# The head of an attention and gated feed-forward kernel, issued in one listed order on all engines

## The chip, the cores and the metric

The kernel runs on one core of one Trainium2 chip. The metric is the device time of the whole launch in microseconds, from the start of the program to its end, as the median of several executions. The core has five engines with a queue of instructions each: TensorE (PE in the profile, with its weight loads as PEld), VectorE (DVE), ScalarE (ACT), GpSimd (POOL) and SyncE (SP), which here issues DMAs. Each engine takes its own instructions in the order in which they stand in its queue, and semaphores hold an instruction until what it reads is there and what it overwrites is no longer needed. The order inside each queue is therefore part of the kernel.

## The reference

Attention with a causal window of 64 over 8 batches, 8 heads, 576 tokens and 64 channels, then a root-mean-square norm and a gated feed-forward layer on the 4608 tokens of 512 channels:

```python
scores = scale * np.matmul(q, k.transpose(0, 1, 3, 2))
rel = pos[:, None] - pos[None, :]
mask = (rel >= 0) & (rel < window)
scores = np.where(mask, scores, -1000000000.0)
...
attn = attn / (np.sum(attn, axis=-1, keepdims=True) + 1e-09)
return np.matmul(attn, v).astype(np.float32)
...
x = np.ascontiguousarray(attn_out.transpose(0, 2, 1, 3)).reshape(B * S, H * D)
rms = np.sqrt(np.mean(x * x, axis=-1, keepdims=True) + 1e-06)
xn = x / rms * rms_g
g = xn @ w_gate
silu = g * (1.0 / (1.0 + np.exp(-g)))
val = xn @ w_val
return (silu * val @ w_out).astype(np.float32)
```

w_gate and w_val have 512 x 1536 elements, w_out 1536 x 512, all f32.

## The kernel before

**Attention.** Two heads make a pair, so that there are 32 pairs, 4 in each batch. Pair n has the tiles q_n and kv_n (keys and values), which SP loads: kv_n by one DMA for the bulk (L348) and two for the last values (L361, L362). A pair's scores come in two parts g = 0 and 1 and two halves, one for each head: sc_n_g_0 and sc_n_g_1 (L397 to L401). Each half uses 64 rows of the PE array. DVE masks the scores and takes their maxima (L414, written to p and st), ACT takes the exponentials (L417), PE turns the weights (tr, L518), ACT or DVE copies them from PSUM (pt, L521 to L523), and PE multiplies them with the values (xp, L536). The result goes to xb. PSUM has one bank for scores, one for tr, two for xp and the widening products, and three (mo) for the feed-forward sums.

**Norm.** After batch 0's four pairs, the sums of squares (ssq) are added up on PE (tot, L773), ten short steps on DVE make inverse roots of them (rm, L791 and L828), and PE spreads these over partitions (rb, L852). DVE scales xb by them and by the weights gsb (L882), and writes xn (L886, L888).

**Feed-forward.** The 4608 tokens are 9 tiles of 512. A product of f32 accuracy is three f16 products of high and low parts (`three`, L976 to L979). Tile 0 runs expert_in(0, c) for the six chunks c of 256 columns: gate sums pg_0_j and value sums pv_0_j for j = 0 to 11, then th and h on ACT, DVE and POOL. expert_out(0) makes the output sums po_0 from h and w_out. Tiles 3 to 8 use a scheme of seven products (L1153).

**Weights.** They arrive as f32 (1 MB a chunk) in staging tiles st_0_c (gate), st_1_c (value) and st_o_c (w_out), issued on SP (L204) into three buffers. ACT makes two exponentials of the top byte (mp, mn, L217 and L218), PE adds them (pw, L226 and L227, with the constant `unit`), DVE puts the other bits in (wt, L229), so that the f32 value is rebuilt. Then come the maxima (top), a scale (n2, z, ws), and the split into high and low f16 parts (L238 to L248) on ACT, DVE and POOL. A staging buffer comes free when DVE's second wt step has read it.

**What sets the order.** SEQ (L1296) is "00 01 02 03 04 05 o0": the six chunks of tile 0, then its output stage o0. Attention of batch 0 (`first_batch`, L727) is written first; attention of batch 1, the widening and the first products of pair 8 are written as a plan of events that `advance` (L1355) calls as tile 0's steps go by. Up to o0 the compiler's own scheduler puts the instructions of each engine in order, by its model of durations. `behind` (L1276) adds edges to that: the parts in it may not be issued ahead of what was last written on the named engines. From o0 on (ORDERED, L46) `in_written_order` (L90) fixes the order on all five engines as it was written.

Of the kernel before, what the change touches and what calls it, by code (L numbers as in the profile page):

```python
# [62 lines left out]

@with_exitstack
def tile_window_attention_moe(
# [205 lines left out]
    def in_scale(c):  # L271
# [7 lines left out]
        nc.vector.tensor_scalar(r.bitcast(I32), n2.bitcast(I32), -0.5, RSQRT_SEED + 12.9 * 2.0**23, ALU.mult, ALU.add)
# [973 lines left out]
    def expert_out(t):  # L1253
        if t == 0:
            pos = [(ps_mo if k < 3 else ps_mi).tile([P, DM], F32, tag="mo" if k < 3 else "mi", name=f"po_0_{k}") for k in range(TT // P)]
            for c in range(NC):
                for k, po in enumerate(pos):
                    tick(Fraction(2, NC))
                    chunk_out(po, t, c, k, c == 0, c == NC - 1)
                    if c == NC - 1:  # L1260
                        store(po, t, k)
            return
        for k in range(TT // P):
            halves = 2 if t == NT - 1 and k == TT // P - 1 else 1
            for e in range(halves):
                es = slice(e * DM // halves, (e + 1) * DM // halves)
                po = (ps_mo.tile([P, DM], F32, tag="mo", name=f"po_{t}_{k}_{e}") if t < FIRST7 else banks[(0, 2, 5, 1)[(k + e) % 4]])[:, es]
                for c in range(NC):
# [4 lines left out]
                    chunk_out(po, t, c, k, c == 0, c == NC - 1, es)
                store(po, t, k, es)

    def behind(parts, engines):  # L1276

        last = {}
        for ins in nc.cur_bb.bb.instructions:
            last[ins.engine] = ins  # L1280
        with ExitStack() as order:
            for e in engines:
                order.enter_context(tc.issue_after(last[e.engine]))
            for part in parts:
                part()
# [145 lines left out]
```

## Time and profile before

| | us |
|---|---|
| median of 3 runs | 988.48 |
| lowest, highest run | 984.96, 990.56 |
| the profiled execution, whole time | 989.32 |
| the profiled execution, span of the profile | 987.2 |
| first output matmul of tile 0 (po_0_0) | 173.4 |

The page divides the span into 40 slices of 24.7 us. Each digit is the share of a slice in tenths; the first seven slices are what comes before o0:

```profile
PE   7778999999999999999999999999999999999998
PEld 5544445444445444588758875886588658847875
DVE  6676966877787775647674766576757645512540
ACT  5566877555544454356635663566366334413440
POOL 3333645487847675557665756675667222200210
PEclk9987999999999999999999999999999999999999
```

A timeline row reads: start, duration, engine, line, operation, output<-inputs with the tile's number left out, size, count, and in brackets the idle time of the engine ahead of it with what ended that time. A product of two f32 tiles is recorded as two matmuls. A windows row reads: start and end, length, busy time and count of each engine, the granted clock of PE as a share of full speed, the busy share of the DMA engines, and GB/s. A group's row ends with busy time, mean ns of one, and idle time ahead of the group with its causes. A row of waits reads: engine and waiting line, what it waited for, us in total, times, the longest. A row of the DMA part ends with the median us from issue to landing.

### The profile page before, as it was taken

The page shows a single profiled execution, that of the slowest core. Times are in us where ns is not written, and L with a number is a line of the kernel's source. Part 1 is how long each engine was busy: PE and PEld are TensorE (multiplying, and loading weights), DVE is VectorE, ACT ScalarE, POOL GpSimd, SP SyncE. Part 2 cuts the span into 40 slices and gives each one's busy share as a digit, 9 for nine tenths or more (in the row PEclk, how much of TensorE's full clock was granted, in tenths as well). Part 3 has the DMA queues.
Part 4 walks back from the last instruction along what each step waited for, and adds up shares of the span by engine and source line. Part 5 has one row for each costly group of instructions (what it writes and reads, how often), then busy time and mean ns, then how long its engine had stood idle before and what let it go on. Part 6 is the DMA issues. An engine that isn't in the chain of part 4 may idle for free.

```text
span 987.2 us, 20767 instructions
## 1 busy us (share of the span) xinstructions
PE 957.8 (97%) x7820; PEld 626.7 (63%) x7831; DVE 631.3 (64%) x1721; ACT 512.3 (52%) x1303; POOL 499.1 (51%) x634
## 2 busy tenths in 40 slices
PE   7778999999999999999999999999999999999998
PEld 5544445444445444588758875886588658847875
DVE  6676966877787775647674766576757645512540
ACT  5566877555544454356635663566366334413440
POOL 3333645487847675557665756675667222200210
PEclk9987999999999999999999999999999999999999
...
GB/s 289 179 95 219 115 255 84 59 160 36 153 124 105 164 213 155 33 147 207 298 35 146 212 294 34 146 219 290 31 197 186 137 33 193 202 76 107 140 8 35
DMA packets 81315, 143.42 MB, mean 145 GB/s; under 512 B 25792, under 2 KB 38336, under 8 KB 81216
## 3 DMA queue, kind: packets, MB, share of 16 engines
...
q8 instruction: 61, 1.00, 0.4%
q10 hardware_dynamic: 576, 1.18, 0.3%
...
HBM read 121.64 MB, written 20.45 MB: 144 GB/s over the span
## 4 chain that ended last, share of the span: by engine, by line
PE 88%; DVE 4%; ACT 2%; POOL 2%; DMA 2%; issue 1%; SPq 0%; POOLq 0%; ACTq 0%; DVEq 0%
PE bk L1153 29%; PE bk L977 6%; PE bk L978 6%; PE bk L979 6%; PE xp L536 5%; PE sc L401 4%; PE po L977 3%; PE po L978 3%; PE po L979 3%; PE pg L979 3%; PE pv L977 3%; PE pg L977 3%; PE pg L978 3%; PE pv L979 3%; PE pv L978 3%
## 5 line engine op out<-in xcount | busy, mean ns | idle before, releaser
L1153 PEld LDWEIGHTS <-wt 128*128 128x128 f16 x3024 | 295.2, 98 | 39.2 <-issue 2.8
L383 POOL TENSOR_TENSOR pm<-pm,st 32x288 f32<-32x288 f32 (+1 forms) x384 | 265.0, 690 | 71.4 <-DVE st L451 26.1
L1153 PE MATMUL bk<-xn,wt 128*128 128x256 f16 x1728 | 207.3, 273 | 0.5 <-DVE u L1223 0.5
L998 POOL TENSOR_TENSOR h<-th,h 128x512 f16<-128x512 f32 x78 | 93.8, 1203 | 170.0 <-ACT h L998 156.5
L1153 PE MATMUL bk<-wt,wt 128*128 128x256 f16 x1224 | 150.3, 273 | 0.3 <-ACT u L1173 0.3
L977 PE MATMUL bk<-wt,h 128*128 128x512 f16 (+1 forms) x300 | 111.3, 371 | 0.0
L978 PE MATMUL bk<-wt,h 128*128 128x512 f16 (+1 forms) x300 | 111.1, 370 | 0.0
L979 PE MATMUL bk<-wt,h 128*128 128x512 f16 (+1 forms) x300 | 111.1, 370 | 0.0
L417 ACT ACTIVATE pm<-pm,st 128x128 f32<-128x128 f32 (+1 forms) x216 | 83.9, 389 | 36.6 <-DVE st L414 35.7
L998 ACT CAST h<-th 128x512 f16<-128x512 f32 x94 | 57.9, 616 | 52.0 <-DVE th L1043 34.7
L1195 DVE SCALAR_TENSOR_TENSOR th<-th,bk 128x256 f32<-128x256 f32 x108 | 44.8, 415 | 50.8 <-ACT th L1185 50.3
L979 PEld LDWEIGHTS <-h 128*128 128x128 f16 x436 | 42.7, 98 | 49.6 <-issue 0.8
L977 PEld LDWEIGHTS <-h 128*128 128x128 f16 x436 | 43.0, 99 | 47.8 <-issue 3.1
L1185 ACT ACTIVATE th<-bk,hsc 128x256 f32<-128x256 f32 x108 | 47.9, 471 | 47.8 <-DVE bk L1219 28.4
L978 PEld LDWEIGHTS <-h 128*128 128x128 f16 x436 | 42.7, 98 | 44.7
L1216 DVE TENSOR_TENSOR bk<-bk,s 128x512 f32<-128x512 f32 x36 | 25.1, 696 | 69.0 <-PE bk L1153 48.4
L401 PE MATMUL sc<-kv,q 64*64 64x128 f32 (+1 forms) x1056 | 56.7, 296 | 8.7 <-DMA q<-q 4.8
L998 POOL TENSOR_TENSOR xn<-xb,xn 128x192 f16<-128x192 f32 (+7 forms) x33 | 25.7, 778 | 74.7 <-ACT xn L953 72.5
L977 PE MATMUL pv<-xn,wt 128*128 128x512 f16 x144 | 54.7, 380 | 2.2 <-ACT wt L241 1.6
L977 PE MATMUL pg<-xn,wt 128*128 128x512 f16 x144 | 55.4, 385 | 0.1
L978 PE MATMUL pg<-xn,wt 128*128 128x512 f16 x144 | 55.1, 383 | 0.1
L979 PE MATMUL pg<-xn,wt 128*128 128x512 f16 x144 | 54.8, 383 | 0.1
...
## 6 DMA issues: line engine op xcount, KB each, us to landing
...
kv<-kv SPq DMA_DIRECT2D x28, 608.0 KB, 4.6
...
```

Source lines behind the costliest of these rows:

```text
L383: nc.gpsimd.tensor_tensor(m[to, :us, fr], p[fr, :us, to], r, ALU.mult)
L401: nc.tensor.matmul(out.rearrange("p (n c) -> p n c", c=D), lhsT=qt[hd, j * D : (j + 1) * D], rhs=halves[hd, :1, :] if j == 0 else halves[h ...
L417: nc.scalar.activation(part, part, AF.Exp, bias=low, scale=-1.0, accum_out=total)
L536: nc.tensor.matmul(xp[hd, c * D : (c + 1) * D], lhsT=vv[j][rows, hd], rhs=w, start=True, stop=True, skip_group_check=True,)
L977: nc.tensor.matmul(acc, lhsT=lh, rhs=rh, start=first, stop=False)
L978: nc.tensor.matmul(acc, lhsT=lh, rhs=rl, start=False, stop=False)
L979: nc.tensor.matmul(acc, lhsT=ll, rhs=rh, start=False, stop=last)
L998: part()
L1153: nc.tensor.matmul(acc[:, i * HT : (i + 1) * HT], lhsT=w[:, i, l, kt, :], rhs=b[:, m, kt, :], start=at_start, stop=kt == 1 and j == 2, ski ...
L1185: nc.scalar.activation(cols, acc[:, :HT], AF.Tanh, scale=th_scale[:, c : c + 1])
L1195: nc.vector.scalar_tensor_tensor(cols, cols, 1.0, acc[:, :HT], ALU.add, ALU.mult)
L1216: nc.vector.tensor_tensor(y, y, kept.pop((c, "s1")), ALU.add)
```

## The change

Every engine call goes through a recorder. `nc` is now an object whose five engines note each call under a name made of the engine's first letter and the name of the tile that it writes, without its last number (t for PE, v for DVE, s for ACT and for SP, g for POOL). At o0 `emit_recorded` issues the noted calls in the order of the list ORDER. For each name the calls keep their own order. `in_written_order` starts at 0, so that this order holds on all five engines from the first instruction on. `behind` is gone; its parts are called plainly. All recorded instructions carry line L211 of the changed kernel.

```diff
+ORDER = """
+v.floor s.q_0 s.kv_0 v.unit s.kv_1 s.q_1 v.unit g.mask s.gsb s.q_2 g.mask*2 s.kv_2 g.mask s.kv_0 g.mask*2 s.st_0_0
+g.mask s.kv_2 g.blocked s.kv_3*2 t.sc_0_0*5 s.kv_1 t.sc_0_0*3 v.p_0_0_0 t.sc_0_0*2 t.sc_0_1 v.p_0_0_0 s.p_0_0_0
...
-    nc = tc.nc
+    recorded = []
+    strict = {"on": False}
...
+            def call(*args, **kw):
+                if strict["on"]:
+                    return real(*args, **kw)
+                out = kw["out"] if "out" in kw else args[0]
+                tile_name = getattr(out, "tensor", out).name.rpartition("_")[0]
+                if self.name == "tensor" and tile_name.startswith("sc_"):
+                    tile_name = tile_name[:-2]
+                recorded.append((f"{self.name[0]}.{tile_name}", partial(real, *args, **kw)))
...
+    def emit_recorded():
+
+        steps = {}
+        for name, step in recorded:
+            steps.setdefault(name, deque()).append(step)
+        for entry in ORDER.split() or [name for name, _ in recorded]:
+            name, _, count = entry.partition("*")
+            for _ in range(int(count or 1)):
+                steps[name].popleft()()
+        assert not any(steps.values())
+        strict["on"] = True
+        return 0 if ORDER else len(tc.nc.cur_bb.bb.instructions)
...
-    def behind(parts, engines):
...
-    behind(
-        [partial(advance, 0)],
-        () if E("NB0", 0) else (nc.vector, nc.scalar, nc.gpsimd, nc.tensor),
-    )
+    advance(0)
     rest(1)
     first_full = 1
     for e in SEQ:
         if e == ORDERED:
-            strict["on"] = True
-            written = len(nc.cur_bb.bb.instructions)
+            written = emit_recorded()
```

The set of instructions of each engine is the same as before. The order differs in the head alone: in the first 1118 of PE's 11892 instructions, 421 of DVE's 1723, 212 of ACT's 1015, 105 of POOL's 639 and 52 of SP's 450.

On DVE, the start of the program: `unit` is the constant of the widening, kv_0 the values of pair 0 that are copied into place, p_0_0_0 the first masked scores. Before:

```order
L119 CAST unit_106<-ident_101 128x128
L120 TENSOR_SCALAR unit_106<-ident_101 128x128
L354 COPY kv_0_157<-kv_0_157 64x512
L355 COPY kv_0_157<-kv_0_157 64x512
L414 ISA p_0_0_0_199,st_0_0_201<-sc_0_0_0_187,blocked_139 128x128
```

and now:

```order
L211 CAST unit_106<-ident_101 128x128
L211 TENSOR_SCALAR unit_106<-ident_101 128x128
L211 ISA p_0_0_0_136,st_0_0_138<-sc_0_0_0_134,blocked_111 128x128
L211 ISA st_0_0_138 128x1
```

The two copies of kv_0 have moved behind the masks of pair 0.

On PE, the scores of pair 0's second part, whose halves are sc_0_1_0 and sc_0_1_1. Before:

```order
L401 MATMUL sc_0_1_0_218<-kv_0_157,q_0_155 64x128 x4
L401 MATMUL sc_0_1_1_219<-kv_0_157,q_0_155 64x128 x4
L401 MATMUL sc_1_0_0_268<-kv_1_161,q_1_159 64x128 x4
L401 MATMUL sc_1_0_0_268<-kv_1_161,q_1_159 64x64
L401 MATMUL sc_1_0_1_269<-kv_1_161,q_1_159 64x128 x4
```

and now, with the first six of the eight:

```order
L211 MATMUL sc_0_1_0_139<-kv_0_125,q_0_124 64x128
L211 MATMUL sc_0_1_1_140<-kv_0_125,q_0_124 64x128
L211 MATMUL sc_0_1_0_139<-kv_0_125,q_0_124 64x128
L211 MATMUL sc_0_1_1_140<-kv_0_125,q_0_124 64x128
L211 MATMUL sc_0_1_0_139<-kv_0_125,q_0_124 64x128
L211 MATMUL sc_0_1_1_140<-kv_0_125,q_0_124 64x128
```

Four matmuls of one half ran after four of the other; now the halves alternate.

On PE, the norm stage: tot is the sum of squares, rb the spread of the inverse roots, pw_0_1 and pw_1_1 the widening of the gate and the value weights of chunk 1, pw_0_2 that of the gate weights of chunk 2. Before:

```order
L773 MATMUL tot_0_657<-one_109,ssq_0_321 128x1 x5
L852 MATMUL rb_0_0_680<-ident_101,rm_0_663 128x128 x4
L226 LDWEIGHTS unit_106
L226 MATMUL pw_0_1_0_697<-mp_0_1_641,unit_106 128x512
```

and now:

```order
L211 MATMUL tot_0_234<-one_107,ssq_0_161 128x1 x5
L211 LDWEIGHTS unit_106
L211 MATMUL pw_1_1_0_253<-mp_1_1_251,unit_106 128x512
L211 LDWEIGHTS unit_106
L211 MATMUL pw_1_1_0_253<-mn_1_1_252,unit_106 128x512
L211 LDWEIGHTS unit_106
L211 MATMUL pw_0_2_0_262<-mp_0_2_259,unit_106 128x512
L211 LDWEIGHTS unit_106
L211 MATMUL pw_0_2_0_262<-mn_0_2_260,unit_106 128x512
L211 MATMUL rb_0_0_238<-ident_101,rm_0_235 128x128 x4
```

The four widening matmuls of pw_0_1, which began behind rb, have moved ahead of tot, and four of pw_1_1 and pw_0_2 between tot and rb. Four more of these two (pw_0_2_1, pw_1_1_1) and the scores sc_4_0 now stand between rb and the first product of tile 0. On POOL, the low part of wt1 stands behind DVE's rm steps in the list.

On SP, the DMAs around kv_4 (keys and values of batch 1's first pair) and the staged weights. Before, kv_4's first DMA was SP's 15th row, and later came:

```order
L204 DMA st_0_2_762<-w_gate 128x4x2048
L348 DMA kv_6_965<-kv 128x1216
L361 DMA kv_6_965<-kv 64x512
L362 DMA kv_6_965<-kv 64x512
L204 DMA st_1_2_785<-w_val 128x4x2048
L204 DMA st_0_3_890<-w_gate 128x4x2048
```

and now:

```order
L211 DMA st_0_2_255<-w_gate 128x4x2048
L211 DMA st_1_1_236<-w_val 128x4x2048
L211 DMA q_4_241<-q 128x576
L211 DMA kv_6_299<-kv 128x1216
L211 DMA kv_5_244<-kv 64x512
L211 DMA st_1_2_261<-w_val 128x4x2048
L211 DMA kv_4_242<-kv 128x1216
L211 DMA st_0_3_285<-w_gate 128x4x2048
```

kv_4's bulk has moved behind the staging of st_1_2, and st_0_2 ahead of st_1_1.

More of the change, by code (lines that the diff above doesn't have):

```diff
@@ L5 @@
 import math
+from collections import deque
 from contextlib import ExitStack
@@ new lines @@
+v.p_0_1_1 v.p_1_0_0 s.p_0_1_1 t.sc_1_1*4 g.p_0_0_0 t.sc_1_1*3 t.tr_0_0_1 s.p_1_0_0 v.st_0_1 t.tr_0_0_1 s.p_1_0_0
+t.tr_0_0_0 g.p_0_0_0 v.st_0_1 t.tr_0_0_0 s.p_1_0_1 t.tr_0_0_0 v.p_1_1_1 g.p_0_1_0 t.sc_2_0 v.p_1_1_0 s.p_1_0_0 v.kv_0
+s.p_1_0_1 g.p_0_1_1 v.p_1_1_0 s.p_1_1_0 v.st_1_0 t.sc_2_0*2 s.pt_0_0_1 t.sc_2_0*6 s.mp_0_0 t.sc_2_0 v.p_2_0_0 v.one
+t.tr_0_1_1 v.pt_0_0_0 t.tr_0_1_1 v.pt_0_0_0 v.kv_0 t.tr_0_1_0*2 v.p_2_0_1 s.q_3 t.xp_0_0 v.kv_2 t.xp_0_0*4 s.p_1_1_1
+v.p_2_0_0 t.xp_0_0*4 v.st_1_0 t.xp_0_0 v.p_2_0_0 s.p_1_1_0 v.pt_0_1_0 g.p_1_0_0 t.sc_2_1 v.p_1_1_1 s.xb_0 t.sc_2_1
@@ new lines @@
+v.kv_3 t.pw_1_0_1 s.p_3_1_0 t.pw_1_0_1 v.st_3_0*2 t.xp_2_0 v.p_3_1_0 t.xp_2_0 s.pt_2_1_1 t.xp_2_0 v.wt3 g.p_3_0_0
+t.xp_2_0*3 s.p_3_1_0 t.xp_2_0*4 t.tr_2_1_0 s.p_3_1_1 t.tr_2_1_0 g.p_3_0_1 s.st_1_1 s.p_3_1_1 v.pt_2_1_0 s.q_4 s.kv_1
+t.tr_3_0_1 v.st_3_1 g.p_3_0_0 t.tr_3_0_1 v.st_3_1 v.top_0 t.xp_2_1*4 s.xb_0 t.xp_2_1 g.p_3_1_0 t.xp_2_1*3 t.tr_3_0_0
+s.mn_0_1 t.tr_3_0_0*2 g.p_3_1_1 v.pt_3_0_0*2 v.top_0 g.ssq_0 s.pt_3_0_1 t.tr_3_1_0*2 s.xb_0 t.xp_3_0*2 s.mp_0_1
+t.xp_3_0*8 v.pt_3_1_0 t.tr_3_1_1*2 v.kv_2 s.kv_6 t.xp_3_1 s.pt_3_1_1 s.kv_5 s.xb_0 v.sq_0 t.xp_3_1*3 g.ssq_0
@@ new lines @@
+t.xp_3_1*4 t.n2_0 t.pw_0_1_0 s.xb_0 v.z_0 t.pw_0_1_0 v.ws_0 s.kv_3 t.pw_0_1_1*2 s.mp_0_2 v.ssq_0 v.wt4 t.tot_0
+s.mn_1_1 v.ws_0 t.tot_0 v.wt4 t.tot_0 v.gpw v.wt3 s.st_1_2 s.mp_1_1 t.tot_0 s.kv_4 t.tot_0 v.gsb s.mn_0_2 v.rm_0*2
+t.pw_1_1_0*2 t.pw_0_2_0 s.wt0 t.pw_0_2_0 v.rm_0*3 s.wt1 v.rm_0*6 v.wt5 v.first_of t.rb_0_0*3 g.wt1 v.wt6 t.rb_0_0
+t.pw_0_2_1*2 v.xb_0 t.pw_1_1_1*2 v.xb_0 v.first_of s.xn_0 v.xb_0 s.xn_0 g.xn_0 s.mp_1_2 v.xb_0 t.sc_4_0 v.wt6 g.xn_0
+t.sc_4_0*6 s.mn_1_2 t.sc_4_0*3 v.p_4_0_0 v.first_of t.pv_0_1 s.st_0_3 v.p_4_0_0 v.first_of t.pv_0_1 v.wt5 t.pv_0_1
@@ new lines @@
+s.kv_4 t.pv_0_1*2 v.p_4_0_1 s.p_4_0_0 t.pv_0_1 v.p_4_0_1 v.first_of s.kv_4 t.pw_1_2_1 v.p_4_0_0 s.p_4_0_1 v.p_4_0_0
+t.pw_1_2_1 v.wt0 s.p_4_0_1 t.rb_0_512 s.st_1_3 t.pw_1_2_0*2 s.p_4_0_0 t.pg_0_1 s.p_4_0_0 t.pg_0_1 v.xn_0 s.xn_0
+t.pg_0_1*2 v.st_4_0 v.xn_0 t.pg_0_1*2 g.xn_0 t.pg_0_0 v.xb_0 t.pg_0_0 v.st_4_0 v.xb_0 s.xn_1 t.pg_0_0 v.xb_0 t.pg_0_0
+s.xn_1 v.xb_0 t.pg_0_0 v.top_1 t.pg_0_0 t.sc_4_1 g.ws_0 t.sc_4_1*7 g.hsc t.pg_0_1 s.mn_0_3 t.pg_0_1 g.p_4_0_0
+v.p_4_1_1 t.pg_0_1 v.p_4_1_0 t.pg_0_1 v.p_4_1_0 t.pg_0_1 g.p_4_0_0 v.p_4_1_1 t.pg_0_1 v.top_1 g.p_4_0_1 s.p_4_1_1
@@ new lines @@
+t.tr_4_0_0*3 s.p_4_1_1 t.pg_0_0 g.hsc t.pg_0_0 s.p_4_1_0 t.pg_0_0 v.sq_1 g.xn_1 v.pt_4_0_0 t.pg_0_0 s.mp_0_3 t.pg_0_0
+v.wt7 t.pg_0_0 t.n2_1 v.pt_4_0_0 t.pv_0_1 v.z_1 t.pv_0_1 v.ws_1 s.th_0_0 v.wt7 t.pv_0_1*3 s.wt2 v.wt5 s.st_0_4
+t.pv_0_1 t.tr_4_0_1 s.kv_6 t.tr_4_0_1 v.th_0_0 t.sc_5_0*5 s.wt3 t.sc_5_0*5 v.top_2 t.pw_0_3_0*2 t.pv_0_0*2 s.th_0_1
+g.wt3 t.pv_0_0*2 v.wt8 s.pt_4_0_1 t.pv_0_0*2 s.xn_1 s.p_4_1_0 v.p_5_0_0 t.pw_0_3_1 v.th_0_1 t.pw_0_3_1 s.mp_1_3
+t.pv_0_0*2 v.wt8 t.pv_0_0*3 v.p_5_0_0 s.st_1_4 s.p_5_0_0 t.pv_0_0 v.st_4_1*2 v.p_5_0_1 t.pv_0_2 s.mn_1_3 v.p_5_0_0
@@ new lines @@
+s.q_6 g.p_4_1_1 t.pv_0_2 v.p_5_0_0 v.p_5_0_1 t.pv_0_2 v.th_0_0 t.pv_0_2 g.xn_1 t.pv_0_2*2 v.wt2 g.p_4_1_0 s.p_5_0_1
+t.tr_4_1_1*2 t.pw_1_3_0 s.pt_4_1_1 t.pw_1_3_0 t.sc_5_1 s.p_5_0_1 t.sc_5_1*4 v.wt9 t.sc_5_1*3 s.p_5_0_0 t.xp_4_0*5
+s.p_5_0_0 t.xp_4_0 v.top_2 t.xp_4_0*3 g.xn_1 t.xp_4_0 s.xn_1 t.tr_4_1_0 s.mp_0_4 t.tr_4_1_0 t.pw_1_3_1*2 t.pg_0_2
+v.sq_2 v.ws_1 t.pg_0_2 v.st_5_0*2 v.p_5_1_1 t.pg_0_2 s.mn_0_4 v.p_5_1_1 g.p_5_0_0 t.pg_0_2 v.p_5_1_0 t.pg_0_2
+v.p_5_1_0 t.pg_0_2 v.pt_4_1_0 t.n2_2 g.p_5_0_1 t.pv_0_2 v.th_0_1 s.h_0_0 t.pv_0_2*2 g.xn_1 v.z_2 t.pv_0_2 s.p_5_1_0
@@ new lines @@
+v.ws_2 g.p_5_0_0 t.pv_0_2 v.wt9 s.xb_1 t.pv_0_2 t.tr_5_0_0 g.ws_1 s.p_5_1_1 v.top_3 t.tr_5_0_0 s.st_o_0 t.tr_5_0_0
+g.h_0_0 s.wt4 t.xp_4_1*8 t.pw_0_4_0*2 v.pt_5_0_0 t.sc_6_0*2 s.p_5_1_1 t.sc_6_0 g.hsc t.sc_6_0 v.pt_5_0_0 t.sc_6_0*4
+v.p_6_0_0 t.sc_6_0 s.p_5_1_0 t.sc_6_0 t.tr_5_0_1 v.wt10 t.tr_5_0_1 t.pg_0_2 s.pt_5_0_1 t.pg_0_2 v.ws_2 v.st_5_1
+t.pg_0_2 v.wt4 s.mn_1_4 g.ws_2 t.pg_0_2*3 t.pw_0_4_1*2 s.xb_1 v.p_6_0_1 t.pg_0_4 v.st_5_1 v.p_6_0_0 t.pg_0_4 s.p_6_0_1
+v.wt7 g.p_5_1_1 t.pg_0_4 s.th_0_2 t.pg_0_4*3 s.mp_1_4 t.xp_5_0 v.th_0_2 t.xp_5_0*8 v.wt10 t.xp_5_0 t.tr_5_1_1*2
@@ new lines @@
+s.mn_o_2 v.p_6_1_1 t.pv_0_5 s.st_1_5 t.pv_0_5 t.tr_6_0_0*3 t.pw_o_2_0 s.h_0_2 t.pw_o_2_0 t.pw_o_2_1 s.p_6_1_0
+t.pw_o_2_1 g.wt6 t.n2_4 s.mn_o_1 t.pv_0_3 v.z_4 t.pv_0_3 v.th_0_3 t.pv_0_3*2 v.wt16 t.pv_0_3 s.mp_o_1 t.pv_0_3
+t.sc_7_0*3 v.pt_6_0_0 t.sc_7_0*6 v.pt_6_0_0 t.sc_7_0 t.pg_0_6 v.wt16 g.hsc t.pg_0_6 s.p_6_1_0 g.hsc t.pg_0_6*2 v.ws_4
+g.h_0_2 v.th_0_5 s.st_o_3 t.pg_0_6 s.wt8 t.pg_0_6 s.kv_7 t.pw_o_1_0*2 t.pg_0_6 v.wt15 t.pg_0_6 s.mp_1_5 t.pg_0_6*2
+v.ws_4 t.pg_0_6 v.wt8 t.pg_0_6 g.ws_4 t.pw_o_1_1 s.p_6_1_1 t.pw_o_1_1 t.pv_0_3 s.mn_1_5 t.pv_0_3 v.wt15 t.pv_0_3*3
@@ new lines @@
+g.hsc s.p_7_1_1 t.pv_0_9 g.h_0_3 v.pt_7_0_0 s.xb_1 t.pv_0_9 v.wt17 t.pv_0_9 s.mp_o_4 t.pg_0_7*2 v.p_7_1_1 v.wt13
+t.pg_0_7*3 s.mn_o_4 t.pg_0_7 v.wt11 t.tr_7_0_1*2 t.pv_0_9*3 s.p_7_1_0 t.pv_0_9 s.p_7_1_1 t.pv_0_9*2 s.pt_7_0_1
+t.pw_o_4_0 v.th_0_9 s.p_7_1_0 t.pw_o_4_0 t.pw_o_4_1 s.kv_6 t.pw_o_4_1 v.st_7_1 v.wt10 t.pv_0_8*2 s.mn_o_5 t.pv_0_8
+g.ssq_1 t.pv_0_8*3 v.wt18 t.pv_0_8 s.mp_o_3 t.pv_0_8*2 v.wt18 t.pv_0_8*3 s.mp_o_5 t.pg_0_10 s.kv_8 g.hsc t.pg_0_10*2
+g.wt11 s.kv_8 t.pg_0_10*2 s.mp_o_4 t.pg_0_10 s.kv_9 t.pw_o_5_0*2 t.pw_o_5_1 s.kv_9 v.wt19 t.pw_o_5_1 t.pg_0_10*2
@@ new lines @@
+s.kv_8 v.th_0_8 t.pg_0_10*3 s.q_9 v.st_7_1 v.wt19 t.pg_0_10 g.p_7_1_1 t.xp_7_0*6 s.mp_o_5 t.xp_7_0*3 g.p_7_1_0
+t.xp_7_0 t.tr_7_1_1*2 t.pv_0_10*2 s.xb_1 t.pv_0_10 v.hsc*2 t.pv_0_10 v.h_0_4 s.th_0_10 t.pv_0_10*2 v.omx*2 t.x0_8
+s.pt_7_1_1 t.x0_8 t.obound s.th_0_7 t.tr_7_1_0*2 t.pv_0_10 v.pt_7_1_0 t.pv_0_10*2 v.oe*2 t.pv_0_10 v.oe*2 v.th_0_7
+t.pv_0_10*2 t.sc_8*2 v.oe t.sc_8 v.os t.sc_8*2 v.hsc t.sc_8*3 v.th_0_10 t.sc_8*2 s.wt13 t.sc_8*6 t.xp_7_1*3 v.hsc
+t.xp_7_1 v.th_0_10 t.xp_7_1*4 t.pv_0_7*2 s.wt12 v.wt13 t.pv_0_7*6 v.wt12 s.wt15 t.pv_0_7*4 t.pg_0_11 s.xb_1 v.th_0_7
@@ L64, in tile_window_attention_moe @@
+t.pg_0_11 s.h_0_4 t.pg_0_11*2 v.wt15 t.pg_0_11 s.kv_7 t.pg_0_11 t.pv_0_11 s.wt14 t.pv_0_11*3 v.ssq_1 t.pv_0_11*2
+s.h_0_5 t.pg_0_11 v.wt14 t.pg_0_11*2 s.wt17 t.pg_0_11 g.h_0_5 t.pg_0_11*2 v.pm_8 t.pv_0_11*2 s.th_0_11 t.pv_0_11*2
+s.wt16 t.pv_0_11 v.th_0_11 t.pv_0_11 g.h_0_4 v.th_0_11 v.pm_8 s.h_0_5 v.wt17 s.h_0_3 g.h_0_5 v.wt16 g.h_0_4 g.h_0_3
+"""
 @with_exitstack
```

62 lines of the change are left out of this document (51 added, 11 removed).

## The prediction

> **What bounds the kernel now.** The page's first part comes first, then a table of five stages up to the first output stage and of the rest.
>
> ```profile
> PE 957.8 (97%) x7820; PEld 626.7 (63%) x7831; DVE 631.3 (64%) x1721; ACT 512.3 (52%) x1303; POOL 499.1 (51%) x634
> core 0: us, PE busy (x) PEld busy (x) DVE busy (x) ACT busy (x) POOL busy (x), PEclk, DMA share, GB/s
> 0.00:4.76 4.76, 0.00 (x0) 0.00 (x0) 0.86 (x11) 1.28 (x1) 2.49 (x14) 1.00 0.62 194
> 4.76:34.20 29.44, 26.98 (x228) 20.00 (x228) 18.87 (x109) 16.96 (x72) 8.95 (x15) 1.00 0.71 252
> 34.20:45.60 11.40, 8.10 (x107) 5.39 (x107) 7.54 (x23) 7.22 (x21) 5.44 (x7) 1.00 0.55 184
> 45.60:58.70 13.10, 6.93 (x35) 5.46 (x36) 10.19 (x23) 6.91 (x9) 4.29 (x5) 0.61 0.53 159
> 58.70:173.40 114.70, 107.51 (x705) 54.72 (x712) 86.13 (x237) 84.76 (x169) 52.15 (x61) 0.96 0.49 157
> 173.40:987.20 813.80, 808.24 (x6752) 541.12 (x6750) 507.70 (x1321) 395.13 (x1034) 425.82 (x533) 1.00 0.43 139
> ```
>
> TensorE (PE) is busy for 957.8 us of a span of 987.2. The order is the same before and after from the first output matmul on, which starts at 173.4. That last row is 813.8 us long with PE busy for 808.24: it is bound by PE, so whatever moves 173.4 moves the end by as much. The change is thus worth what it does to the **head**, the first 173.4 us. There PE is busy for 26.98 + 8.10 + 6.93 + 107.51 = 149.5 us and idle for 23.9. In the same five rows DVE has 123.6 us and ACT 117.1.
>
> Busy time itself isn't fixed. The score matmuls show it, first by group in the windows 4.76–34.2 and 58.7–173.4, then as stretches of the timeline (a product of two f32 tiles is two records):
>
> ```profile
> L401 PE MATMUL sc<-kv,q 64*64 64x128 f32 (+1 forms) x144 | 14.6, 417 | 7.2 <-DMA q<-q 4.8 <-DVE st L414 2.5
> L401 PE MATMUL sc<-kv,q 64*64 64x128 f32 (+1 forms) x167 | 14.3, 294 | 1.5 <-issue 1.0 <-DVE xb L882 0.4
> 65.17 0.65 PE L401 MATMUL sc<-kv,q 64*64 64x128 f32 x8
> 196.69 1.04 PE L401 MATMUL sc<-kv,q 64*64 64x128 f32 x30
> 18.62 1.52 PE L536 MATMUL xp<-pt,kv 64*64 64x64 f32 x18
> 85.80 0.69 PE L536 MATMUL xp<-pt,kv 128*64 128x64 f32 x16
> ```
>
> At 65.17, where the matmuls of one half of the heads follow one another, a record costs 0.65 / 8 = 0.081 us. At 196.69, where the two halves alternate, it costs 1.04 / 30 = 0.035. The last two rows are the values' matmuls with 64 columns: 0.084 us each at 18.62 and 0.043 at 85.80. I read the first 30 us of PE work as running at half speed, although the table has the clock at 1.00 there (no change of it is recorded before 34.2).
>
> **The change part by part.** No instruction is added or removed: each engine issues the same ones. Four things in their order cost or save time.
>
> 1. **The start.** Here PE's second piece of scores waits for the first masks on DVE:
>
> ```profile
> 4.76 2.18 PE L401 MATMUL sc<-kv,q 64*64 64x128 f32 x28 [4.76 <-DMA q<-q]
> 7.72 0.42 DVE L354 COPY kv<-kv 64x512 f32<-64x512 f32 x1 [5.82 <-DMA kv<-kv]
> 8.61 0.29 DVE L414 CUSTOM_DVE_ANT_0 p<-sc,blocked 128x128 f32<-128x128 f32 x1
> 9.40 4.49 PE L401 MATMUL sc<-kv,q 64*64 64x128 f32 x44 [2.46 <-DVE st L414]
> ```
>
> DVE stood 5.82 us in front of two copies of kv_0's values, whose DMA had not landed, and the first mask (8.61) was queued behind them. The new list has the masks ahead of the copies. The first scores are done soon after 4.76, so the masks can run while PE goes on. PE's 2.46 us of idle go: **−2.5**. What is late next is the second mask, 0.29 us long each, against a PE that is still slow; between nothing and 2.46, I take all of it. The copies stay hidden, since values are first multiplied at 18.62.
>
> 2. **Batch 0's scores** alternate between the halves. At half speed I set an alternating record at 2 × 0.035 = 0.069: 144 × 0.069 = 10.0, which is 4.6 less than the 14.6 of the row. If alternation costs 0.035 even there, the gain is 14.6 − 5.0 = 9.6; if masks on DVE (18.87 of 29.44 us busy) hold PE instead, it is about nothing. PE is 26.98 of 29.44 busy in that stage, so a shorter PE stream shows: I take **−5**.
>
> 3. **The norm stage.** One of PE's waits, the timelines around it, and the group of widening matmuls in 58.7–173.4:
>
> ```profile
> PE rb L852 <- DVE rm L828: 4.2, 1, 4.2
> 47.74 2.21 PE L773 MATMUL tot<-one,ssq 128*128 128x1 f32 x10 [0.63 <-DVE z L279]
> 50.09 2.13 POOL L242 TENSOR_TENSOR wt<-wt,wt 128x1024 f16<-128x1024 f32 x1 [0.51 <-ACT wt L241]
> 50.19 2.05 DVE L828 TENSOR_SCALAR rm<-rm 128x5 int32<-128x5 int32 x1
> 52.27 0.16 DVE L828 TENSOR_TENSOR rm<-rm 128x5 f32<-128x5 f32 x1
> 54.18 2.05 PE L852 MATMUL rb<-ident,rm 128*128 128x128 f32 x8 [4.23 <-DVE rm L828]
> 57.86 0.86 PE L401 MATMUL sc<-kv,q 64*64 64x128 f32 x10
> 58.65 0.39 PE L977 MATMUL pg<-xn,wt 128*128 128x512 f16 x1
> L226 PE MATMUL pw<-mp,unit 128*128 128x512 bf16 x16 | 6.6, 410 | 0.0
> ```
>
> PE waits 4.23 us for a chain of rm steps on five numbers per row, then 1.6 us more before 57.86. Eight widening matmuls (pw) now stand inside these waits, at a mean of 0.41 us: up to 3.3 us of PE work that came later before (sc_4_0 moves into the second wait as well, but ran ahead of 58.65 already). One rm step took 2.05 us, where the next took 0.16; it started 0.10 us after POOL's subtraction of wt and ended 0.02 behind it. In the new list that POOL step (wt1) stands behind the rm chain: 1.9 us may go as well. Up to 5.2 us, and nothing at worst, if widening matmuls wait for ACT's exponentials ahead of rb: I take **−2**.
>
> [...]
>
> 4. **The stage 58.7–173.4**, where dense products of tile 0 run between attention of batch 1 and widening. PE is idle for 7.2 of its 114.7 us. The clock was granted in half for two stretches:
>
> ```profile
> 78.60:85.40 6.80, 6.66 (x49) 4.17 (x48) 6.41 (x25) 3.57 (x10) 0.42 (x1) 0.50 0.72 238
> 88.80:92.20 3.40, 3.40 (x9) 1.18 (x8) 1.35 (x10) 0.36 (x1) 3.32 (x5) 0.50 1.00 324
> 92.30:173.40 81.10, 78.41 (x521) 39.52 (x525) 58.61 (x155) 63.29 (x117) 39.03 (x41) 1.00 0.46 148
> PE tr L518 <- DVE pt L523: 2.2, 1, 2.2
> PE pv L977 <- ACT wt L241: 1.6, 1, 1.6
> ```
>
> At full clock the 6.66 + 3.40 us of busy PE would be half, so up to 5 us can go. The scores (167 records, 14.3 us) at 0.035 would be 5.8, so up to 8.5 go. Waits hold at most 7.2. Together up to 20.7; at worst nothing, since DVE (86.1) and ACT (84.8) have their own strict order now. I take **−8**: 5 of the 8.5 on scores, the two long waits of the last two rows as 3, and no gain on the clock, because transposes and widening with their waits still surround the dense blocks.
>
> Sum: −2.5 − 5 − 2 − 8 = −17.5. The profiled execution took 989.32 us (0.8 over the median of 988.48), so 989.3 − 17.5 = 971.8, **972 us**.
>
> What is moved on SP is its DMAs, and no cost is counted for them; the cover is three staging buffers ahead of their use. If that cover is gone, it is the second rival.
>
> **The rivals.** (a) **DVE and ACT become the bound in stage 4.** For it: 86.1 and 84.8 us of busy time, which is 81% and 79% of the 106.7 us that the forecast leaves. If a strict order leaves each waiting for the other, stage 4 gains nothing and the norm stage little: only the start and part of the scores remain, −2.5 − 4 = 983. Against it: the alternated scores spare PE time without asking anything of either.
>
> (b) **Slower: kv_4 behind a weight on SP.** In the new list kv_4's DMA stands on SP behind st_1_2, which must wait for a staging buffer until DVE has widened wt4's second half, and on PE sc_4_0 stands ahead of every dense product.
>
> ```profile
> 61.78 1.27 DVE L229 SCALAR_TENSOR_TENSOR wt<-st,pw 128x512 int32<-128x512 int32 x2
> 63.12 0.37 SPq L204 DMA_DIRECT2D st<-w_val  x1
> kv<-kv SPq DMA_DIRECT2D x28, 608.0 KB, 4.6
> ```
>
> If that widening ended at 63.05, as before, the weight's issue ends at 63.5, kv_4's at 63.9, and it lands 4.6 later, at 68.5. Then sc_4_0 starts there and not at 57.86: +10.6, 989.3 + 10.6 = 1000. It decides as soon as wt4's second half ends after about 52 (57.9 − 4.6 − 0.8 = 52.5). Against it: the list puts wt4 on DVE in front of the rm chain, which began at 50.0 and would begin earlier.
>
> (c) **The clock stays at half for longer.** Windows 47.9–58.1 ran at half with PE busy for little over half of the time:
>
> ```profile
> 47.90:58.10 10.20, 5.75 (x23) 4.46 (x26) 7.55 (x17) 5.30 (x6) 3.69 (x5) 0.50 0.44 152
> 92.49 0.38 PE L979 MATMUL pg<-xn,wt 128*128 128x512 f16 x1
> 89.32 0.63 PE L977 MATMUL pg<-xn,wt 128*128 128x512 f16 x1
> ```
>
> If shorter scores leave PE less busy in 34.2–45.6, its 8.10 us double in part there: +6 to 8 us against the forecast, 972 + 7 = 979. The row of a dense product is 0.63 long at half and 0.38 at full clock. [...]
>
> (d) **The change does nothing**: PE would have been held by arrivals of q, kv and weights at the same times. Against it: 2.46 us of the start are DVE's order and not a DMA's.
>
> **How the numbers follow.** The forecast (963 to 980, with c inside its upper edge) has 0.60. A fully dense head has 0.10: idle cut to about 5 us and the larger gains on scores and clock, 149.5 − 5 − 10 − 5 + 4.8 + 5 = 139.3, or 34 below, 955. (a) at about 983 has 0.13, (d) within half a per cent 0.07, (b) and its kin 0.10. The range reaches from 960 to 986: down to half of what lies between the forecast and the dense head and somewhat beyond, up to the start gap alone (−2.5 to −3). It leaves out (b), (d) and about half of the dense case. Faster by over 0.5% (about what a measurement of this kernel can tell from no change, 4.9 us) has 0.60 + 0.10 + 0.13 = 0.83, within it 0.07, slower 0.10.
>
> **What would show it.** Step 1: the first mask before 7 us and no wait of 2.46 on st. Step 2: score records of batch 0 at 0.07 or less and the dense block's start some 9 us earlier than 58.65. Step 3: rm's first step at 0.2 us, pw in front of rb. Step 4: the first output matmul about 156, PE idle below 5 us in the stage. A sc_4_0 that waits for kv's DMA would make me wrong, and so would a longer tail than 813.8.

## The result, and the profile after

| kernel | median, us | lowest to highest | ratio to before (95% interval) |
|---|---|---|---|
| before | 988.69 | 984.96 to 990.56 | |
| changed | 965.67 | 964.22 to 965.95 | 0.9769 (0.9739 to 0.9799) |

The change makes the kernel 23.0 us faster; 17.5 were forecast. The profiled execution of the changed kernel took 965.56 us. These are the first row of its page, its stages (cut at the same events: first score, first scale matmul n2, first dense product, first output matmul), and the windows at half clock that the profile records, in the form of the tables of before:

```profile
PE 942.9 (98%) x7831; PEld 615.2 (64%) x7831; DVE 622.3 (65%) x1721; ACT 511.9 (53%) x1303; POOL 500.1 (52%) x634
4.84:42.49 37.65, 31.61 (x335) 20.72 (x335) 25.92 (x134) 26.24 (x94) 14.11 (x22) 0.94 0.78 275
42.49:54.53 12.04, 9.29 (x54) 5.57 (x53) 9.49 (x29) 10.22 (x12) 4.20 (x3) 0.76 0.42 145
54.53:150.50 95.97, 93.98 (x696) 47.75 (x695) 81.98 (x230) 82.89 (x169) 47.76 (x60) 1.00 0.60 189
150.50:963.70 813.20, 808.05 (x6751) 541.19 (x6749) 504.53 (x1326) 391.31 (x1029) 431.49 (x537) 1.00 0.42 138
38.10:44.90 6.80, 6.60 (x48) 4.18 (x48) 3.63 (x8) 4.50 (x9) 2.42 (x2) 0.50 0.70 258
48.30:51.80 3.50, 3.28 (x12) 2.26 (x12) 2.41 (x8) 1.86 (x3) 1.60 (x1) 0.51 1.02 404
```

The tail is 813.2 us long, where it had 813.8: the head's gain comes through whole. The first output matmul starts at 150.5 and not at 173.4. Of these 22.9 us only 4.1 are made by the first dense product (54.53, before 58.65). The other 18.8 are made in the stage of dense products, 114.77 us before and 95.97 now (other executions of the order of before have about 111.7 there, as the experiments show, so that 15.7 to 18.8 is the fairer figure). PE is 98% busy in it, DVE and ACT 85% and 86%, and the clock is at full speed all through; before, 10.2 us of that stage were at half.

Here are PE's busy times in that stage by tile, of before and then of the changed kernel: scores, gate sums, value sums.

```profile
58.65:173.42 114.77, 14.13 (x168) 9.20 (x166) 10.38 (x44) 0.96 0.49 157
58.65:173.42 114.77, 37.46 (x144) 8.11 (x12) 8.16 (x12) 0.96 0.49 157
58.65:173.42 114.77, 35.49 (x144) 8.21 (x12) 0.96 0.49 157
...
54.53:150.50 95.97, 6.80 (x158) 4.63 (x156) 10.29 (x40) 1.00 0.60 189
54.53:150.50 95.97, 34.50 (x144) 7.64 (x12) 8.13 (x12) 1.00 0.60 189
54.53:150.50 95.97, 33.88 (x144) 7.58 (x11) 1.00 0.60 189
```

Scores take 7.3 us less, the same 288 dense matmuls 4.6 less (3.0 and 1.6), and PE's idle time falls from about 7.2 to 2.0. That is 17.1 of the 18.8; the rest is in other matmuls and in the eight widening ones that now run ahead of the stage.

### The profile page after: what moved, and what is told of

It is laid out like the page before. It is cut to its first block, busy times and chain, and to the rows that moved or that the text cites. A ratio compares the mean times of both kernels' runs of the same rounds, so it can differ in the third digit from the quotient of the medians.

```text
span 963.7 us, 20769 instructions
## 1 busy us (share of the span) xinstructions
PE 942.9 (98%) x7831; PEld 615.2 (64%) x7831; DVE 622.3 (65%) x1721; ACT 511.9 (53%) x1303; POOL 500.1 (52%) x634
## 4 chain that ended last, share of the span: by engine, by line
PE 88%; DVE 6%; POOL 2%; issue 2%; ACT 1%; DMA 0%; POOLq 0%; DVEq 0%; ACTq 0%
PE bk L181 49%; PE po L181 10%; PE pv L181 7%; PE pg L181 6%; PE xp L181 4%; PE pv L211 2%; PE pg L211 2%; PE sc L181 2%; PE sc L211 1%; DVE th L181 1%; POOL pm L181 1%; DVE wt L211 1%; PE xp L211 1%; PE tr L211 1%; PE rb L181 1%
## 5 line engine op out<-in xcount | busy, mean ns | idle before, releaser
L181 PEld LDWEIGHTS <-wt 128*128 128x128 f16 x3624 | 353.3, 98 | 109.3 <-issue 4.2
L181 PE MATMUL bk<-wt,h 128*128 128x512 f16 (+1 forms) x900 | 191.1, 371 | 0.0
L181 PE MATMUL po<-wt,h 128*128 128x512 f16 x408 | 90.7, 379 | 0.0
L181 POOL TENSOR_TENSOR xn<-xb,xn 128x448 f16<-128x448 f32 (+7 forms) x45 | 37.6, 843 | 85.4 <-ACT xn L181 83.0
L181 PE MATMUL pg<-xn,wt 128*128 128x512 f16 x288 | 66.1, 379 | 0.0
L181 ACT ACTIVATE ot<-bk,hsc 128x512 f32<-128x512 f32 (+1 forms) x25 | 16.7, 670 | 63.5 <-PE bk L181 63.5
L181 DVE CUSTOM_DVE_ANT_0 pm<-sc,blocked 128x128 f32<-128x128 f32 x191 | 48.8, 282 | 1.0 <-PE sc L181 1.0
L181 DVE SCALAR_TENSOR_TENSOR th<-bk,th 128x256 f32<-128x256 f32 x108 | 45.8, 424 | 3.7
L211 PEld LDWEIGHTS <-wt 128*128 128x128 f16 x288 | 27.6, 99 | 30.9 <-DVE wt L211 0.5
L181 ACT CAST xn<-xb 128x448 f16<-128x448 f32 (+7 forms) x56 | 23.8, 430 | 42.2 <-DVE xb L181 42.1
L181 DVE STREAM_TRANSPOSE pm<-pm 128x512 f32<-128x512 f32 (+1 forms) x72 | 39.6, 554 | 7.9 <-POOL pm L181 7.9
```

The costliest lines, as they stand in the source:

```text
L181: return real(*args, **kw)
L211: steps[name].popleft()()
```

## The experiments

Twelve kernels. Each holds another list in the changed kernel's recorder (no_list an empty one; warm20, keep and both add matmuls). Where the halves of a score part are moved apart, each has its own name (sc_0_0_0 and sc_0_0_1 for sc_0_0). Ratios are to the kernel before in the same series, whose median lay between 987.06 and 988.86. The changed kernel was measured in its own series alone, and its interval overlaps with that of each kernel from serial_halves down in this table. Differences of 1 to 2 us among these are therefore read from medians and traces, and are not certain.

| kernel | median, us | ratio (95% interval) |
|---|---|---|
| listed_before | 986.34 | 0.9991 (0.9975 to 1.0007) |
| no_list | 991.35 | 1.0039 (1.0023 to 1.0054) |
| after_then_before | 983.33 | 0.9964 (0.9947 to 0.9982) |
| before_then_after | 976.07 | 0.9889 (0.9873 to 0.9905) |
| before_alt | 987.69 | 1.0009 (0.9995 to 1.0022) |
| serial_halves | 963.06 | 0.9752 (0.9734 to 0.9770) |
| serial0 | 963.72 | 0.9750 (0.9729 to 0.9770) |
| apart | 967.81 | 0.9795 (0.9775 to 0.9815) |
| copies_first | 967.68 | 0.9801 (0.9781 to 0.9820) |
| warm20 | 964.54 | 0.9763 (0.9740 to 0.9785) |
| keep | 963.59 | 0.9751 (0.9733 to 0.9770) |
| both | 961.64 | 0.9737 (0.9721 to 0.9753) |

### The list or the recorder

listed_before writes down the order of before as a list; no_list empties the list:

```diff
-ORDER = """
-v.floor s.q_0 s.kv_0 v.unit s.kv_1 s.q_1 v.unit g.mask s.gsb s.q_2 g.mask*2 s.kv_2 g.mask s.kv_0 g.mask*2 s.st_0_0
...
+ORDER = ""
```

> The list holds the order that the kernel before had up to the output stage, engine by engine, issued through the same recorder (one mask of pair 8 stands later on DVE). If the order alone makes the difference: 988, within 3 us, first output matmul at 172 to 175. If dropping the old edges or the recorder brings something by itself: 980 or below.

> The changed kernel with an empty list: the calls are issued as written and the compiler's scheduler orders the head, without the edges of before. If the list is what brings the gain: 980 or above. If dropping the edges is enough: 970 or below.

Recorder and strictness bring nothing by themselves (0.9991), and without the list the scheduler does a little worse than with the old edges (1.0039). The gain is in the order. listed_before shows something else as well: its stage of dense products was shorter, in the same order as before (but for one mask of pair 8 on DVE).

```profile
58.69:170.35 111.66, 105.06 (x714) 53.75 (x713) 85.70 (x230) 84.57 (x168) 52.11 (x60) 0.98 0.49 162
79.50:82.90 3.40, 3.32 (x30) 2.31 (x33) 3.40 (x8) 2.38 (x7) 0.00 (x0) 0.50 0.79 263
```

The stage lasts 111.66 us (before 114.77), with 3.4 us at half clock where before had 10.2. So 6.8 us less at half clock go with 3.1 us less time. The executions of the kernel before agree: those with a mean granted clock of 0.993 had a median of 986.2 us (11 of them), those with 0.989 one of 989.6 (7). The profile of before is of the second kind, so that some 3 us of what separates it from the changed kernel are not the order's.

### The two halves of the list

Both hybrids are cut at the first dense product. The list of the one starts as the changed list and goes on with the order of before; the other is the reverse:

```diff
 t.pw_0_2_1*2 v.xb_0 t.pw_1_1_1*2 v.xb_0 v.first_of s.xn_0 v.xb_0 s.xn_0 g.xn_0 s.mp_1_2 v.xb_0 t.sc_4_0_0 v.wt6 g.xn_0
 t.sc_4_0_1 t.sc_4_0_0 t.sc_4_0_1 t.sc_4_0_0 t.sc_4_0_1 t.sc_4_0_0 s.mn_1_2 t.sc_4_0_1 t.sc_4_0_0 t.sc_4_0_1 v.p_4_0_0
+v.first_of*3 s.kv_4*2 s.q_6 s.kv_6*2 g.ws_0 g.hsc*2 v.wt0 t.pg_0_0 t.pv_0_0 t.pg_0_1 s.xn_0 t.pg_0_0*3 t.pv_0_0*3
...
```

> The changed order up to the first product of tile 0, then the order of before for all that is left of the head. If the gain is made where the profile shows it (first dense product 4.1 us earlier with eight widening matmuls more behind it): 982 to 985. Rival: the early part prepares the late one (weights staged earlier, clock open), and most of the gain stays: 975 or below.

> The order of before up to the first product of tile 0, then the changed order for what is left (the load of q_8 moved behind that of q_7 so that its buffer is free). If the late stage makes its gain by itself: 965.7 + 4 to 6 = 970 to 972. Rival: it needs the early part's staging and clock: 978 or above.

The early part alone is worth 3.7 us (987.06 to 983.33), the late part alone 11.0 (976.07), a result between the two that were expected. Of the whole, 23.0 in its own series and 21.4 against the 987.06 of this one, 7 to 8 belong to neither. Where they go shows in the timeline of before_then_after between rb and the first dense product:

```profile
54.41 2.05 PE L212 MATMUL rb<-ident,rm 128*128 128x128 f32 x8 [4.29 <-DVE rm L212]
58.09 0.89 PE L212 MATMUL sc<-kv,q 64*64 64x128 f32 x10
61.92 0.59 PE L212 MATMUL pw<-mp,unit 128*128 128x512 bf16 x1 [2.94 <-ACT mp L212]
65.39 0.76 PE L212 MATMUL sc<-kv,q 64*64 64x128 f32 x10
66.08 1.47 PE L212 MATMUL pv<-xn,wt 128*128 128x512 f16 x6
```

With the norm stage of before, PE waits 4.29 us for rm, and all that the changed list does inside that wait comes behind it: a wait of 2.94 us for ACT's exponentials, the eight widening matmuls and half of sc_4_0. The first dense product starts at 66.08, 7.4 us later than in before (58.65). The rest of the head is then as fast as in the changed kernel (66.08 to 160.60, 94.5 us). So leaving the norm stage unfilled costs the changed list 7.4 us. In the other hybrid the filled stage puts the first dense product at 52.38, but the old order behind it takes nearly as long as it did (114.77):

```profile
52.38:165.68 113.30, 103.30 (x697) 52.43 (x695) 81.96 (x229) 79.99 (x164) 53.41 (x63) 0.95 0.46 152
```

### Alternation, or neighbouring halves

serial_halves issues, in every part, one half wholly behind the other; serial0 does so in pairs 0 to 3 alone; before_alt alternates in the order of before:

```diff
-g.mask s.kv_2 g.blocked s.kv_3*2 t.sc_0_0*5 s.kv_1 t.sc_0_0*3 v.p_0_0_0 t.sc_0_0*2 t.sc_0_1 v.p_0_0_0 s.p_0_0_0
+g.mask s.kv_2 g.blocked s.kv_3*2 t.sc_0_0_0*5 t.sc_0_0_1*5 s.kv_1 v.p_0_0_0 t.sc_0_1_0*4 t.sc_0_1_1*4 v.p_0_0_0
```

> The changed kernel, with the score matmuls of one half behind those of the other in each part, as many of them stood before; all else as in the changed list. If steps 2 and 4 of the prediction price alternation rightly (5 us each, and the score rows fell by 10.3 us in all): 965.7 + 10 = 976, about half of it before the first dense product. Rival: in batch 0 DVE's masks and the clock set the pace, not the score stream (72 score records were done at 13.8 in both kernels): 971 or below, all of it behind the first dense product.

> The order of before through the list, and the two halves of a score part alternate wherever that part stood in one piece on PE (pairs 0 to 3 but for two parts; none of batch 1). By step 2 of the prediction: 5 us below the listed order of before, 983. Rival (masks and clock set the pace of batch 0): within 2 us of it, 986 to 989.

> The changed kernel with one half behind the other in the score parts of batch 0 alone (pairs 0 to 3); batch 1 and pair 8 alternate as in the changed list. If the 2.6 us that the version with all parts serial gained come from the start, where two alternating halves need two free PSUM banks at once and PE waited 2.3 us in six places for masks: 962 to 963.5, first score part of pair 1 done by 12. If that gain was the phase of the clock's windows: 965 to 966.

The answers go against step 2. Alternation brought the old order nothing (1.0009): its 144 score records of batch 0 took 14.16 us, those of before 14.55. Without it the changed order is no slower but, by the medians, 2.6 us (serial_halves) and 1.9 us (serial0, 0.2 above its range) faster; their intervals overlap with the changed kernel's, so that this gain is likely but not shown. First the starts of PE in the changed kernel, with its row of waits for the masks, then the start of serial_halves:

```profile
4.84 1.13 PE L211 MATMUL sc<-kv,q 64*64 64x128 f32 x16 [4.84 <-DMA q<-q]
6.50 0.90 PE L211 MATMUL sc<-kv,q 64*64 64x64 f32 x6 [0.53 <-DVE st L211]
12.09 1.73 PE L211 MATMUL sc<-kv,q 64*64 64x128 f32 x16 [0.38 <-DVE st L211]
PE sc L211 <- DVE st L211: 2.3, 6, 0.5
...
4.81 4.92 PE L208 MATMUL sc<-kv,q 64*64 64x128 f32 x56 [4.81 <-DMA q<-q]
10.21 1.72 PE L208 MATMUL sc<-kv,q 64*64 64x128 f32 x16
```

The first 72 score records are done at 13.82 (12.09 + 1.73) in the changed kernel, at 13.89 in before (9.40 + 4.49) and at 11.93 in serial_halves. By then the changed list has lost 1.8 us to five waits for masks (the sixth of the row comes at 81.38, in the dense stage) and has run the product gps (0.37 us), which came later before: nearly all that it had won from the one wait of 2.46. The halves of a part have a PSUM tile each; a likely reason, not tried, is that an alternating part needs two free ones at once.

How much a half costs depends on its neighbour. The first row is serial_halves late in batch 0, the second a part of batch 1 there whose second half did not run beside its first, and the third the changed kernel; the last two are parts of 20 records, serial_halves and then the changed kernel:

```profile
26.73 0.68 PE L208 MATMUL sc<-kv,q 64*64 64x128 f32 x16
58.16 1.31 PE L208 MATMUL sc<-kv,q 64*64 64x128 f32 x16
73.15 0.67 PE L211 MATMUL sc<-kv,q 64*64 64x128 f32 x16
64.08 1.04 PE L208 MATMUL sc<-kv,q 64*64 64x128 f32 x20
66.69 0.77 PE L211 MATMUL sc<-kv,q 64*64 64x128 f32 x20
```

Sixteen records in 0.68 us with one half queued behind the other, 0.67 alternating: the chip ran the second half beside the first although it stood behind it. Eight records alone took 0.65 in before, at 65.17. Parts of 20 records overlap only in part that way (1.04 against 0.77), but serial_halves' dense stage is no longer for it (95.70 us against 95.97). Most of the price is that of standing alone, which apart puts back: in seven parts of batch 1 it moves the first half six dense matmuls ahead.

```diff
-t.pg_0_0 t.sc_4_1 g.ws_0 t.sc_4_1*7
+t.sc_4_1_0*4 t.pg_0_0 v.xb_0 t.pg_0_0 v.st_4_0 v.xb_0 s.xn_1 t.pg_0_0 v.xb_0 t.pg_0_0 s.xn_1 v.xb_0 t.pg_0_0 v.top_1
+t.pg_0_0 t.sc_4_1_1*4
...
```

> The changed kernel, and in seven score parts of batch 1 (all but the first) the two halves are pulled apart on PE, six dense matmuls between them, each half of four or five in a row. Theory now: a half alone takes 0.65 us and two neighbouring halves together 0.68, whatever their order, so that pulling apart costs 7 x 0.6 = 4 us: 969 to 971. Rival: the late stage is not bound by PE's score stream and takes it in: 965 to 967.

```profile
90.54 0.65 PE L215 MATMUL sc<-kv,q 64*64 64x128 f32 x8
93.17 0.66 PE L215 MATMUL sc<-kv,q 64*64 64x128 f32 x8
53.04:151.75 98.71, 96.89 (x688) 51.04 (x696) 82.20 (x230) 83.19 (x169) 47.59 (x60) 1.00 0.58 184
```

Each half of such a part costs 0.65 again, the scores take 10.97 us of the stage (6.80 in the changed kernel), and the stage lasts 98.71 us, 2.7 more than the changed kernel's; the median is 2.1 higher, below the 969 to 971 that were expected. In the profile the seven parts thus cost some 0.4 us each, about two thirds of the 0.6.

### The copies at the start

```diff
-t.sc_0_0*5 s.kv_1 t.sc_0_0*3 v.p_0_0_0
+t.sc_0_0*5 s.kv_1 t.sc_0_0*3 v.kv_0 v.kv_0 v.p_0_0_0
```

The two entries further down the list are gone.

> The changed list with the two copies of kv_0's values again ahead of the first masks on DVE. By step 1 of the prediction the wait of 2.5 us comes back and costs as much: 968. Rival: the gap before was filled by later waits for masks, so that nothing is lost by 14 us: 965 to 966.5.

```profile
8.91 0.86 DVE L211 COPY kv<-kv 64x512 f32<-64x512 f32 x2 [7.23 <-DMA kv<-kv]
10.15 0.90 PE L211 MATMUL sc<-kv,q 64*64 64x64 f32 x6 [3.97 <-DVE st L211]
```

The median rises by 2.0 us (965.67 to 967.68). DVE stands 7.23 us in front of the copies, PE 3.97 in front of the masks. The first dense product starts at 56.65 (54.53 in the changed kernel), and the stage behind it is as long as there (95.94 us). So step 1 priced the wait about rightly, if it is taken out of this order.

### The clock

warm20 issues 20 matmuls of the constant ahead of the first scores; keep puts 21 into three waits late in batch 0. Nothing reads their sums. This is keep's addition; its list says where they run:

```diff
+        for name, count in (("idle0", 21),):
+            idle = ps_mi.tile([P, TT], F32, tag="mi", name=name)
+            for _ in range(count):
+                nc.tensor.matmul(
+                    idle[:, :256], lhsT=unit[:, 0, :], rhs=unit.rearrange("p a b -> p (a b)"), start=True, stop=True
+                )
```

> The changed kernel with 20 matmuls of the constant unit (128 x 256, bf16) ahead of the first scores, whose sums nothing reads. PE is idle there until 4.84. If half clock is what makes batch 0's PE work long and DVE doesn't bound it: the clock opens by 8 us, stays open until 24, and 3 to 8 us go: 958 to 963. Rival: the f32 work on half of the array lets the clock fall back, or DVE's masks bound batch 0: 964 to 967.

> The changed kernel with 21 matmuls of the constant unit (128 x 256, bf16, sums that nothing reads) in three waits of PE late in batch 0 (6 ahead of xp_2_0, 8 ahead of tr_3_0_1, 7 ahead of tr_3_1_0). If PE's thinning there is what closes the clock at 38.1, it stays open past 45 and the 6.8 us at half cost 2 to 3 us less: 962.5 to 964. Rival: the norm's chain on DVE sets the time to the first dense product: 965 to 967.

Windows of warm20, then of keep:

```profile
6.90:10.30 3.40, 2.17 (x41) 1.30 (x36) 2.21 (x20) 2.32 (x11) 0.00 (x0) 1.00 0.95 323
10.30:24.00 13.70, 12.58 (x120) 8.26 (x112) 8.52 (x56) 9.01 (x36) 5.41 (x10) 0.50 0.56 212
24.00:44.50 20.50, 15.14 (x189) 10.04 (x191) 17.68 (x67) 18.32 (x54) 8.68 (x12) 1.00 0.81 272
...
24.90:45.40 20.50, 16.72 (x207) 11.86 (x210) 17.68 (x66) 18.08 (x50) 8.68 (x12) 1.00 0.77 263
45.40:48.80 3.40, 3.08 (x10) 1.71 (x10) 2.86 (x13) 3.34 (x4) 0.00 (x0) 0.50 0.87 291
```

Behind the constant matmuls the clock was open by 8.6 us (14 score records there took 0.66 us), but it closed at 10.3 and stayed at half till 24 while PE was busy for 12.58 of 13.70 us: busy time as the profile counts it didn't hold the clock. The median fell by 1.1, and the intervals overlap. In keep the clock stayed open until 45.4, where the changed kernel's fell at 38.1, and the median fell by 2.1 to 963.59, within the range of the first theory. That the constant matmuls did it isn't shown. In apart, whose order is the changed kernel's up to the first dense product, the clock stayed open until 44.5 without them, and in warm20, which has none in these waits, until 44.5 too. The first dense product started at 52.84 in keep, 53.03 in apart and 54.53 in the changed kernel: one order comes with more than one course of the clock, and the 2.1 us are hardly more than that. For the theory speaks the mean granted clock of the executions: 0.998 in four of keep's five, 0.991 to 0.996 in the changed kernel's four (0.993 to 0.998 in apart's).

### Both together

The list of serial0 with the matmuls of keep, and four more ahead of tr_2_0_0.

> The order of serial0 (halves one behind the other in pairs 0 to 3) together with the constant matmuls of keep in the same three waits, and four more ahead of tr_2_0_0. If the two gains (about 2 us each against 965.7) are separate, the start by the banks and the later stretch by the clock: 961 to 962.5. If both are the same gain (when the clock opens and closes): 963 to 964.5.

961.64 us, 4.0 below the changed kernel and in the range of two separate gains, though which of the two brings what stays open. Its start has no wait for a mask:

```profile
5.02 4.92 PE L215 MATMUL sc<-kv,q 64*64 64x128 f32 x56 [5.02 <-DMA q<-q]
```

Its first dense product starts at 50.94, earlier than in any other kernel here. By the medians it is the fastest of the study, 0.9737 of before.

## Why the prediction held, point by point

The sign, the place (all in the head, the tail unchanged) and the range were right: 965.67 lies between 960 and 986. The forecast of 972 was 6.3 us too high, and that it came so near is in part luck: steps 1 to 3 were to bring 9.5 us by the first dense product and brought 4.1, step 4 was to bring 8 and brought 18.8.

**Step 1, the start, −2.5.** The wait went as described, and putting it back costs 2.0. But it was not a gain on its own: the alternation of step 2 took it back by 13.8 us.

**Step 2, alternation in batch 0, −5.** This step was wrong, and the reading that failed is the one from 65.17 and 196.69, "where the two halves alternate, it costs 0.035". The row at 65.17 is one half alone among dense products; what it lacks is a neighbour, not alternation. In batch 0 the halves stood side by side already, so that there was nothing to win (before_alt, 1.0009, with 14.16 us for the records that the step put at 10.0). The 11.3 us that they take in the changed kernel are no gain of alternation either, since serial0 has 11.3 without it. By the times of like records the clock opened earlier: at 24.5 in the changed kernel (a widening matmul takes 0.63 us at 23.32 and 0.38 at 25.16), and by 20.3 in serial_halves (0.38 at 20.29), whose list is serial0's up to sc_4_0; in before it opened at 34.2. In the changed list alternation made the first 72 records 1.9 us later (13.82 against 11.93), as much as the medians differ by (serial0).

**Step 3, the norm stage, −2.** The mechanism was right. PE's wait of 4.23 for rm shrank to 0.22:

```profile
46.79 0.17 DVE L211 TENSOR_SCALAR rm<-rm 128x5 int32<-128x5 int32 x1
48.90 2.04 PE L211 MATMUL rb<-ident,rm 128*128 128x128 f32 x8 [0.22 <-DVE rm L211]
52.86 0.43 PE L211 MATMUL sc<-kv,q 64*64 64x128 f32 x2 [0.59 <-DMA kv<-kv]
```

The rm step that took 2.05 beside POOL's subtraction takes 0.17 without it. In each of the five kernels whose POOL subtraction of wt runs inside the rm chain, one rm step lasts about 2 us, whichever stands beside it (2.05 in before; in no_list another step than in before, 2.04 from 53.73 on, beside 2.12 from 53.63 on). In the nine others no rm step is that long (0.16 to 0.17 us each in the changed kernel). Nor is every DVE step long beside that subtraction: in the changed kernel three xb steps ran beside it in 2.08 us, 0.69 each (in before, four behind it in 2.72, 0.68 each). No kernel put POOL's step back alone, so that its share of the gain isn't shown. The stage from n2 to the first dense product is no shorter (12.04 us, before 11.93) since it holds the eight widening matmuls, which are missing from the next stage. So the term of 2 shows up in step 4; the changed list with the norm stage of before reaches the first dense product 7.4 us later than before does (before_then_after).

**Step 4, the dense stage, −8.** It gave 18.8 between the two profiles and 15.7 against listed_before. Here the term that was mis-sized most is the clock, put at nothing: no part of the stage ran at half, and the dense matmuls alone became 4.6 us shorter. That is the late list's doing: in all nine kernels with the changed list (or one near it) behind the first dense product the granted clock of the stage is 1.00 and its length 94.5 to 98.7 us, in the five with the order of before there, or the scheduler's, 0.95 to 0.98 and 111.2 to 114.8 (how much of it is at half varies, as listed_before shows). listed_before puts the price at 3.1 us for 6.8 us of half clock, so that 10.2 us are worth between 4 and 5. The scores were put at 5 and gave 7.3 of busy time, some of it the clock's; apart puts 4.2 of it back, and 2.7 us of the stage. The waits were put at 3 and gave 5.2; the two that the step names (2.2 and 1.6) are gone. How much of the stage each of these is worth by itself was not tried.

**The rivals.** (a) DVE and ACT did not become the bound, though they are 85% and 86% busy now. (b) The wait for kv_4, one of the signs of being wrong, came, but was 0.59 us: kv_4's load went out behind st_1_2 at 46.4, and wt4's second half was done at 45.8, far ahead of 52. (c) went the other way: from the first score on, about 50 us were at half clock in the head of before and about 30 now, since it opened at 24.5 and not at 34.2. Up to there the profile notes no half clock in either kernel; it is read from the times of like records, in before 14 value matmuls in 1.12 us at 30.24 and in 0.68 at 34.33. Other executions agree: 24 to 25 in apart, keep and warm20, about 35 in listed_before and 37 in before_alt. The 4.1 us by the first dense product are all made in that stretch: both kernels stand equal at 13.8, the changed one reaches n2 at 42.49 (before 46.72), and no kernel parts the clock there from the rest of the order. The profile's busy time does not decide when the clock opens: 26.98 busy us of 29.44 did not open the clock in before, nor 12.58 of 13.70 in warm20. What opens it stays open.
